# Linear attention and a routed MLP on one core: query transpositions on copied fp32r tiles, stacked tail keys, a new order table

## Chip, cores, metric

One core of a Trainium2 chip runs the whole program in one launch. The metric is device time in microseconds, as the median of several executions. The core has TensorE (PE; its weight loads are listed as PEld), VectorE (DVE), ScalarE (ACT), GpSimd (POOL) and SyncE (SP), which issues most DMAs.

## The reference

Eight heads of linear attention over eight sequences of 576 tokens, then a layer of eight experts in which each token goes to the one expert with the largest gate value:

```python
def phi(x):
    proj = np.einsum('bhsd,df->bhsf', x, w_phi)
    proj = proj - np.max(np.abs(proj), axis=-1, keepdims=True)
    return np.concatenate([np.exp(proj), np.exp(-proj)], axis=-1)
q_p, k_p = phi(q), phi(k)
kv = np.einsum('bhsf,bhsd->bhfd', k_p, v)
z = np.sum(k_p, axis=2)
num = np.einsum('bhsf,bhfd->bhsd', q_p, kv)
den = np.einsum('bhsf,bhf->bhs', q_p, z)[..., None] + 1e-06
x = (num / den)  # tokens x 512
expert_idx = np.argmax(x @ w_gate, axis=1)
for e in range(8):
    h = np.maximum(x[expert_idx == e] @ w1[e], 0.0)
    out[expert_idx == e] = gate_w[...] * (h @ w2[e])
```

All inputs and outputs are fp32.

## The kernel before

**Precision.** Products that must be exact to fp32 are made of fp32r operands: a tile is split into a high part (rounded to fp32r, written by ACT mostly) and a low part (the rest, written by DVE or POOL), and three products are added: high x high, high x low, low x high. Other products (`pn`, `pf`) and the transpositions take fp32 operands.

**Attention.** The work is cut into 16 units: four groups `g` of two sequences, and in each four pairs `pr` of heads. The tokens of a unit are nine pieces of 128 columns: eight of one sequence each and a ninth (number 8, the tail) that holds the last 64 tokens of both sequences. They are worked on in five steps, `PIECES`: the tail, then (0,1), (2,3), (4,5), (6,7). For each step and for `k` and `q`:

- `load` (L234) brings `xr` by an SP DMA, `split_high` and `split_low` make `xh` and `xl`; `project_steps` (L257) makes three products of 256 columns per piece into `ps_proj`; `project_max` (`mx`) and `project` (`t`, L282) are two DVE instructions.
- For keys, `k_features` (`e`), `k_high` (`kh`) and `k_low` (`kl`) follow on ACT, and on DVE or POOL.
- For queries, `q_turn_steps` (L315) transposes `t` in 128x128 blocks on PE into `pt`, as fp32, and `q_features` takes the exponentials of `pt` into `qp` or `qz` on ACT.
- `kv_steps` (L367) adds up `pk`, 65 output rows x 256 columns, over five pieces of one sequence `bb`, for two heads, with three products each (`kh` with `vh`, `kh` with `vl`, `kl` with `vh`): 30 per sequence and 60 per unit. For the tail piece the values of the other sequence are zero.
- `kv_copy`, `fold_steps` (`pf`), `num_steps` (`pn`, 73 columns, or 146 from the tail's `qz`), `normalize` and `store` end the unit.

**The order.** Each step of a unit has a letter (capitals for odd units), and the strings `HEAD`, `GROUP` and `TAIL` are the order in which all steps of all units are written into the program; each engine takes its share in that order. PE, DVE, ACT, POOL and SP all issue in order, and a step that waits holds what is behind it on its engine. The pools rotate their buffers.

**Experts.** Rows of `x_dram` are gathered in blocks of 128 (`xg`), transposed on PE into `px` (`x_parts`, L1128, four per block), split, and multiplied by `w1` (`pm`) and `w2` (`po`). 17 units take two blocks of one expert, the others one.

Of the kernel before, what the change touches and what calls it, by code (L numbers as in the profile page):

```python
# [12 lines left out]
I32 = mybir.dt.int32  # L13
# [52 lines left out]

@with_exitstack
def tile_linear_attention_moe(
# [18 lines left out]
    ident = keep.tile([P, P], F32, name="ident")  # L87
    make_identity(nc, ident)
# [13 lines left out]
    sm = late.enter_context(tc.tile_pool(name="sm", bufs=2, side="right"))  # L102
    sg = late.enter_context(tc.tile_pool(name="sg", bufs=1, side="right"))
    ps_kv = late.enter_context(tc.tile_pool(name="ps_kv", bufs=2, space=PSUM, side="right"))
    hold = mid.enter_context(tc.tile_pool(name="hold", bufs=1, side="right"))
    ps_nm = mid.enter_context(tc.tile_pool(name="ps_nm", bufs=2, space=PSUM, side="right"))
    inp = early.enter_context(tc.tile_pool(name="inp", bufs=1, side="left"))
    work = early.enter_context(tc.tile_pool(name="work", bufs=1, side="left"))
    kvp = early.enter_context(tc.tile_pool(name="kvp", bufs=1, side="left"))
    ps_pr = early.enter_context(tc.tile_pool(name="ps_pr", bufs=2, space=PSUM, side="left"))  # L110
    ps_tr = early.enter_context(tc.tile_pool(name="ps_tr", bufs=2, space=PSUM, side="left"))


    w_bd = const.tile([P, 2 * F], F32, name="w_bd")
# [4 lines left out]
    V.tensor_tensor(w_lo, w_bd, w_hi, op=ALU.subtract)  # L119


    one20 = const.tile([P, 2 * NC + 2, 1], F32, name="one20")
    V.memset(one20, 0.0)
    V.memset(one20[:, 0 : 2 * NC - 2], 1.0)
    V.memset(one20[0:D, 2 * NC - 2 : 2 * NC], 1.0)
    V.memset(one20[D:P, 2 * NC : 2 * NC + 2], 1.0)
# [22 lines left out]
    fold_parts += [lambda h=h: G.tensor_copy(fold[:, h, 0 : D + 1], ident[0 : D + 1, 0 : D + 1]) for h in range(H)]  # L149
# [27 lines left out]
    sel_p = rt.tile([P, NTILE, P], BF16, name="sel_p")  # L177
# [27 lines left out]
    CHUNKS = ((8, 0, 1, 2, 3), (4, 5, 6, 7, 8))  # L205
# [95 lines left out]
    def k_high(st, c0, n):  # L301
        m = 2 * n
        kh = kvp.tile([P, m, 2, F], F32R, name="kh", tag=f"kh{n}", bufs=3 * n - 1)
        A.copy(kh, st["e", c0][:, 0:m])
        st["kh", c0] = kh

    def k_low(st, c0, n):
        m = 2 * n
        kh = st["kh", c0]
        kl = kvp.tile([P, m, 2, F], F32R, name="kl", tag=f"kl{n}", bufs=3 * n - 1)  # L310
# [56 lines left out]
    def kv_steps(st, bb):  # L367


        def step(hh, i, c, j):  # L370
            vh, vl = v_tiles[st["u"] % 2]
            if (hh, i, j) == (0, 0, 0):
                st["pk", bb] = ps_kv.tile([P, 2, 2 * F], F32, name="pk", tag="pk")
            n = D if j == 1 else D + 1
            c0 = c if c == 8 else c - c % 2
            s0 = 2 * (c - c0)
# [3 lines left out]
                st["kl" if j == 2 else "kh", c0][:, s0 + hh].rearrange("p s f -> p (s f)"),  # L380
                start=(hh, i, j) == (0, 0, 0),
                stop=(hh, i, j) == (1, 4, 2),
# [6 lines left out]
            for j in range(3)  # L389
# [119 lines left out]
    def unit_items(st):  # L509
# [11 lines left out]
        for x in "kq":  # L521
            for c, n in PIECES:
# [97 lines left out]
    def route(g, lgc, c0, n, final=None):  # L620
# [96 lines left out]
        def count_step(c):  # L717
            oh_b, base_b = r["oh_b"], r["base_b"]
# [8 lines left out]
            else:  # L727
                T.matmul(r["prk"], ones, base_b.unsqueeze(1).to_broadcast([P, n, E]), start=False, stop=True)
# [190 lines left out]

    q_tail = [hold.tile([P, 2, 2, 2, D], F32, name=f"qz{i}") for i in range(2)]  # L920
# [7 lines left out]
    for g in range(NG):  # L928
# [9 lines left out]
    }  # L938
    HEAD = (
        "a0gb20B000000c0e212ahjd2g2ikk2jfjl2bk2D2n222m2pFKoKcssgtjje2haK22dMbjijjOqjljjuujfjjjhSSnATilkpkkkkn"  # L940
        "kGrckkkqkmkeuuuukopuurAjjjjCjjssslqsuEuuumuuutuunuuurapjjjjjjoduuuuqluufuuuunJJvJsuuLHrsBJwNsJJJJJJP"
        "JLJJJJwQsLwwICuNuuupuuNuuuukxkktJJkyUyyqRUgkkyEmyPUUuuyoUUyryaQsssysJJJtJJJLJJJJycULRyuuPuNuuuuuNuuu"
        "uuQuuuyUeKKPKKKKkkMUkUvkURkAUQkUwUUwUDmUwRUUhwOUUyUUoyUUPyxUsszsszyFzUKtKKUzyUKUyQiUbKKKKMKKVKKSyMcU"
        "SyUUOSWUSOWRSTGSSSjjjjjTljjjjnUWUlUpjjjejjnjqWUUXUpUKKlKbYUKrUYdUKUnYUqKfUYMUUYUpjjOUYUjrUAYCUjjUYqu"
        "jjjljjjjUdYluUEYuUnYuUYnuVuyuupfyauuWukkuHWruBkkkkkkkqWumIWumuyupuyXuyouyussoqySyukzrkgkzkkzkuCYSzum"
        "(YSyuZyouySyrZuTZyuyZuyuytSSzSSzvYzuEuzYzTszzY(zuYsYuYBuYsYuYsY(utJYuJYuJJJLJJJJNYuLYPuJYZuNJYQ(uJJZ"
        "YPRsJYuJZkwDukZYL)sQwuFkNwuYskPwuYxRsakkktkmkkkkyumYcuyouuQyueuoyuyuZyZuyZsZyZuRAJJJu)ysJuyZsZvJZJJJ"
        "hLJJJJUwL)sswtsUNiwsUyNsUPwUUxyUUyUtUyUKzK)UzyDzUGKKKKQzKMFKKUyOUUMPySSKRKbKOKyTUKKUyQMUUyUUyOUcUyRU"
        "UyUUyUUyUVUySUySUyeUSzyzUjzjSyUTzUy(UjjbjljjjjnUWUlUpjjjynUjqjjydlSKUWUprKySKnfWUyqUKWSKXUypASrKzKKz"
        "KMKKKTYzUUzYzUzzU(YzOCUUYUYMqUEYUYSOYUjj(jUYrSajUYSVjjjjHjljjjuWlSSWTSunIW(SuYnSupWuuXYuuYuTuYukZkuZ"  # L950
        "YgdZukkkkqZkmfkkuYouumpYsskrkBkokYtukkuYqmuuYuuYouCuYruuYuuYuuYuvuYsuYsuYEusZYZuJZJsYutZuY)uJJBJLJJ"
    )
    GROUP = (
        "JJNuwuLuPJJJYNuJQJJYDLskuwuPRkYskNFwuYQukwskxuYPasRkZkkZkmkkktyZuuZyZuZZu)yZocuuyuymQueyuy3syuJJ)Juy"
        "soAJuysvRJJJJhJJJJUwLsswtsLUiw)sUyNsUDwUUNytUUyxUUyU3PKKUFyGUKzK3KK4K4KQzK3Uy5zbU5UyUzPU3yRUMUyUMUyU"
        "QUyOUUOySSKK3TKKRKKycUMUyUUyOUVUySUySUy5UeSz7yzUjzjSyUTzUy(Ujjbjljjj7jnUWUlUpjjjynUjqjjydl7SKUWUprKy"
        "SKnfWUyqUK7WSKXUypASrKzKKzKMKKKTYzUUzYzUzzU(YzOCUUYUYMqUEYUYSOYUjj(jUYrSajUYSVjjjjHjljjjuWlSSWTSunIW"
        "(SuYnSupWuuXYuuYuTuYukZkuZYgdZukkkkqZkmfkkuYouumpYsskrkBkokYtukkuYqmu66uYu6o666666C6uYru3uY3uuYuuY4u"
        "uYuuY4suY5suY4usZY5ZuJZJs4Yu5ZuY)uJ4JJ5LJJJJNuvY5uLu4JJJY5NuJtJJw5sLkuwDuk5YNsPkwu5YPukwFskxuYQskZkk"
        "ZQkmkkkEyBZuuZyZtuZZu)yZouuyaucymuyuy4RsyuJRoJ)PJuysJuysJvJJJLJ4JJJUwLesDswsUNtw)sUyNsUwFtUAUxyUUyUU"  # L960
        "PyUbKzKUzyzUKQKKKzKMKKUyOQUURySSKKTKKyURMK4KUyUMUyPUUyOUUyUOUcyUUyQUeUyUUySVUySUhRybUSzyzUjzjSyUTzUy"
        "(UjjjljjjijnUWUlUpjjjynUjqjjydlSKUWUpKnfyGSKWUyqUKWSrKAUySXrKpKKzKMKKKYzUOTUYUUYzUzUzYCzUzY(zUMYqUYE"
        "SYOUjjjUYSjU(rYSVjajjjHjjjljuWSSlWTSuIWSnuYSudnW(uuYTuXuYuuYupkZkuZfYgZukkkkpZkmkkuYoBuumYqsskkkokYt"
        "ukrkuYqmuuYuuYouCuYuuYuuYruuYuvuYsuYsuYusZYZuJZJEsYutZuY)uJJJLJJB"
    )
# [445 lines left out]
```

## Time and profile before

| what | value |
|---|---|
| runs | 912.37, 911.63, 907.03 us; median 911.63 |
| the profiled execution | 909.77 us, of which its span 908.1 us |
| TensorE (products) | 882.9 us busy, 6703 instructions |
| TensorE (weight loads) | 824.9 us busy |
| DVE, ACT, POOL | 589.5, 611.2, 487.3 us busy |
| mean granted clock | 0.987 |

The span runs from the first to the last instruction of one execution. Products on PE overlap, so the busy time of PE says how often it had something in flight, and the distance between starts says what one product cost. All instructions of engines that are recorded for ordering carry line 59, that of the helper; the names of their tiles tell them apart. A row of the timeline may stand for several equal instructions (x2, x4).

### The profile page before, as it was taken

Reading aid. Unit: us, or ns where it says so; the run is one execution under the profiler, and the core shown is the slowest. Engines: PE = TensorE matmul, PEld = TensorE weight load, DVE = VectorE, ACT = ScalarE, POOL = GpSimd, SP = SyncE. Lnnn points to the kernel's source line nnn. Section 1 sums busy time; section 2 is a strip of 40 time slices with the busy share of each in tenths; the row PEclk is TensorE's granted clock in tenths of the full one; section 3 lists DMA queues with packets and bytes.
Section 4 is the critical chain, followed back from the end, with each engine's and each line's share of the span. In section 5 each row is a group of like instructions: output and inputs, shape, how many; then the busy total and the mean of one; then the engine's idle time right before and its main releaser. Section 6 shows DMA issues by size and latency. Waiting matters only on the chain. (4 is left out here: it accounts for less than half of the span.)

```text
span 908.1 us, 18331 instructions
## 1 busy us (share of the span) xinstructions
PE 882.9 (97%) x6703; PEld 824.9 (91%) x6703; DVE 589.5 (65%) x1075; ACT 611.2 (67%) x954; POOL 487.3 (54%) x332
## 2 busy tenths in 40 slices
PE   8999999999999999999999999999999999999994
PEld 6999999999999999998889999999999999987883
DVE  7777788787877788868754444444444444457950
ACT  7987888887898778844745555555555555568951
POOL 6976666776695677632543333333333333337641
PEclk8999999999999999999999999999999999999997
DMA  5243333333333341251342253522434634653100
GB/s 171 89 130 109 109 108 99 88 96 108 109 91 93 101 109 54 87 199 21 101 163 70 94 163 116 163 70 87 139 125 132 219 118 141 228 206 120 46 24 16
DMA packets 64621, 102.46 MB, mean 113 GB/s; under 512 B 10702, under 2 KB 28622, under 8 KB 64528
## 3 DMA queue, kind: packets, MB, share of 16 engines
q1 hardware_dynamic: 57136, 80.31, 28.4%
q0 software_dynamic: 6720, 20.80, 7.4%
q8 instruction: 54, 0.88, 0.4%
q14 instruction: 39, 0.32, 0.1%
q10 hardware_dynamic: 672, 0.15, 0.1%
HBM read 136.81 MB, written 20.26 MB: 173 GB/s over the span
## 5 line engine op out<-in xcount | busy, mean ns | idle before, releaser
L59 DVE TENSOR_TENSOR wl<-raw,wh 128x1024 fp32r<-128x1024 f32 x138 | 184.6, 1350 | 139.9 <-ACT wh L59 135.6
L59 ACT CAST wh<-raw 128x1024 fp32r<-128x1024 f32 x184 | 191.2, 1050 | 94.3 <-PE po L59 67.3
L59 POOL TENSOR_TENSOR wl<-raw,wh 128x1024 fp32r<-128x1024 f32 x46 | 113.4, 2470 | 172.2 <-ACT wh L59 167.0
L59 PE MATMUL pn<-kf,qp 128*128 128x73 f32 x1024 | 167.2, 251 | 0.2 <-DVE kf L59 0.2
L59 PE MATMUL pm<-xh,wh 128*128 128x256 f32 x544 | 154.6, 284 | 1.5 <-DVE hl L59 1.5
L59 PE MATMUL pm<-xl,wh 128*128 128x256 f32 x544 | 154.9, 285 | 1.2 <-DVE xl L59 1.2
L59 PE MATMUL pm<-xh,wl 128*128 128x256 f32 x544 | 154.7, 284 | 0.0
L59 PEld LDWEIGHTS pn<-kf,qp 128*128 128x128 f32 x1024 | 154.1, 189 | 0.5 <-DVE kf L59 0.4
L59 PE MATMUL po<-wh,hh 128*128 128x512 f32 x328 | 131.4, 401 | 0.3 <-ACT hh L59 0.3
L59 PE MATMUL po<-wl,hh 128*128 128x512 f32 x328 | 128.6, 392 | 0.0
L59 PE MATMUL po<-wh,hl 128*128 128x512 f32 x328 | 128.0, 391 | 0.6 <-DVE hl L59 0.6
L59 POOL TENSOR_TENSOR xl<-xr,xh 128x512 fp32r<-128x512 f32 (+2 forms) x63 | 91.6, 1456 | 61.0 <-ACT xh L59 57.3
L59 POOL TENSOR_TENSOR kl<-e,kh 128x1024 fp32r<-128x1024 f32 x47 | 112.7, 2406 | 20.0 <-ACT kh L59 10.9
L59 DVE TENSOR_REDUCE mx<-ps_proj 128x4 f32<-128x512 f32 (+1 forms) x160 | 99.9, 630 | 26.0 <-PE ps_proj L59 25.1
L59 PEld LDWEIGHTS pm<-xh,wh 128*128 128x128 f32 x544 | 104.9, 193 | 4.2 <-DVE hl L59 1.7
L59 PEld LDWEIGHTS pm<-xl,wh 128*128 128x128 f32 x544 | 104.9, 193 | 4.1 <-DVE xl L59 1.7
L59 PEld LDWEIGHTS pm<-xh,wl 128*128 128x128 f32 x544 | 104.8, 193 | 0.0
L59 DVE TENSOR_TENSOR t<-ps_proj,mx 128x512 f32<-128x512 f32 (+1 forms) x160 | 99.5, 634 | 5.5 <-ACT e L59 0.9
L59 PE MATMUL pk<-kh,vh 128*65 128x256 f32 x320 | 98.1, 307 | 0.5 <-ACT kh L59 0.5
L59 PE MATMUL pk<-kl,vh 128*65 128x256 f32 x320 | 97.7, 305 | 0.1
L59 PE MATMUL pk<-kh,vl 128*64 128x256 f32 x320 | 97.6, 305 | 0.0
L59 POOL DMA_INDIRECT out<-ob,sidx x41 | 44.5, 1086 | 91.1 <-ACT ob L59 81.2
(201 smaller groups left out, 2006.1 us busy)
## 6 DMA issues: line engine op xcount, KB each, us to landing
raw<-w SPq DMA_DIRECT2D x184, 512.0 KB
vt<-vv SPq DMA_DIRECT2D x15, 640.0 KB
x_dram<-xrow SPq DMA_DIRECT2D x30, 256.0 KB
xr<-qT SPq DMA_DIRECT2D x15, 320.0 KB
xr<-kT SPq DMA_DIRECT2D x15, 320.0 KB
xr<-kT SPq DMA_DIRECT2D x17, 256.0 KB
xr<-qT SPq DMA_DIRECT2D x17, 256.0 KB
x_dram<-xrow SPq DMA_DIRECT2D x32, 32.0 KB
```

The lines of the kernel that those rows point to most:

```text
L59: m = f(*a, **kw)
```

## The change

- Queries: a new step `q_move` (letters `[` and `]`) copies `t` into a tile `tq` by an SP DMA, and `q_turn_steps` transposes `tq` instead of `t`, with operands read as fp32r, through a helper `turn`. The gathered rows `xg` are transposed by `turn` too. The identity is written as fp32r.
- Tail keys: `k_stack_steps` (letters `{` and `}`) makes two tiles `ka`, one per sequence, by four SP DMAs: the sequence's 64 rows of `kh` stand on its own half of the partitions and its 64 rows of `kl` on the other. The host puts the tail values twice into `vv`, once on each half. For the tail, `kv_steps` then needs two products per head (`ka` with `vl`, `ka` with `vh`) instead of three.
- Order: `HEAD`, `GROUP` and `TAIL` are new, `GROUP` is used twice; the last 42 steps instead of 51 are spread into the first expert unit.
- Buffers: pools of the attention part are wrapped in `Ring`, in which a table names the buffer of each tile. There is one more pair of `kh` and `kl` buffers of two pieces.
- Some tiles of the index computation lie in a pool `spots`, opened when the pool `hold` is closed.

```diff
+class Ring:
+    def tile(self, shape, dtype, name, tag=None, bufs=None):
...
+        slots = self.slots.get(tag, "")
+        slot = slots[k] if k < len(slots) else k % n
+        return self.pool.tile(shape, dtype, name=name, tag=f"{tag}_{slot}", bufs=1)
...
-    CHUNKS = ((8, 0, 1, 2, 3), (4, 5, 6, 7, 8))
+    CHUNKS = ((0, 1, 8, 2, 3), (4, 5, 6, 7, 8))
...
+    def k_stack_steps(st):
+
+        def step(b, i):
+            if i == 0:
+                st["ka", b] = kvp.tile([P, 2, 2, F], F32, name="ka", tag=f"ka{b}", bufs=2)
+            own, other = (slice(D * x, D * x + D) for x in (b, 1 - b))
+            dst, src = (other, "kl") if i else (own, "kh")
+            return SP.dma_start(st["ka", b][dst], st[src, 8].bitcast(F32)[own])
+
+        return [lambda a=(b, i): step(*a) for b in range(2) for i in range(2)]
+
+    def q_move(st, c0, n):
+        m = 2 * n
+        st["tq", c0] = work.tile([P, 4, F], F32, name="tq", bufs=2)
+        SP.dma_start(st["tq", c0][:, 0:m], st["t", "q", c0][:, 0:m])
+
+    def turn(dst, src):
+
+        return T.transpose(dst.bitcast(F32R), src.bitcast(F32R), ident_r)
+
...
-            return T.transpose(st["pt", c0][:, i, :], st["t", "q", c0][:, i, :], ident)
+            return turn(st["pt", c0][:, i, :], st["tq", c0][:, i, :])
...
+            if c == 8:
+                keys = st["ka", bb].bitcast(F32R)[:, hh]
...
-            for j in range(3)
+            for j in ((1, 0) if c == 8 else range(3))
...
+        "tq": "01010110100101010101010101010101010101010101010101010101010101010101010101010101",
...
-            T.transpose(px[:, k, :], xg[:, k * P : (k + 1) * P], ident)
+            turn(px[:, k, :], xg[:, k * P : (k + 1) * P])
```

Where the order moves instructions: first PE, in a unit of the steady part. Before, transpositions into `pt` stand between single `pf`, `pn` and `pk` products:

```order
L59 MATMUL pk<-kh,vh_166 65x256
L59 MATMUL pf<-fold,kvT 128x73
L59 MATMUL pt<-ident,t 128x128 x2
L59 MATMUL pf<-fold,kvT 128x73
L59 MATMUL pt<-ident,t 128x128
L59 MATMUL pk<-kh,vl_168 64x256
L59 MATMUL pf<-fold,kvT 128x73
L59 MATMUL pt<-ident,t 128x128
L59 MATMUL pk<-kl,vh_166 65x256
L59 MATMUL pn<-kf,qp 128x73
L59 MATMUL pt<-ident,t 128x128
L59 MATMUL pk<-kh,vh_166 65x256
```

Now, at the like place:

```order
L59 MATMUL pk<-kh,vl_166 64x256
L59 MATMUL ps_proj<-w_lo,xh 128x256
L59 MATMUL pt<-ident_r,tq 128x128 x4
L59 MATMUL pk<-kl,vh_164 65x256
L59 MATMUL pk<-kh,vh_164 65x256
L59 MATMUL pf<-fold,kvT 128x73
L59 MATMUL pk<-kh,vl_166 64x256
L59 MATMUL pf<-fold,kvT 128x73
L59 MATMUL pk<-kl,vh_164 65x256
L59 MATMUL pf<-fold,kvT 128x73
```

The four transpositions of a pair of pieces stand together, and every `pf` now has a `pk` behind it. Up to the last `pn`, 260 of 296 transpositions are followed by another one or by a `pk`; before, 119 were.

Then SP, in the steady part. Before, its queue holds loads of `xr` and `vt` and stores of `xrow`:

```order
L59 DMA xr<-kT 128x640
L59 DMA x_dram<-xrow 64x128
L59 DMA vt<-vv 128x1280
L59 DMA xr<-qT 128x640
L59 DMA x_dram<-xrow 128x4x128
L59 DMA xr<-qT 128x512
L59 DMA x_dram<-xrow 64x128
L59 DMA xr<-kT 128x512
```

Now the copies stand between them:

```order
L59 DMA xr<-qT 128x512
L59 DMA x_dram<-xrow 128x4x128
L59 DMA ka<-kh 64x512
L59 DMA xr<-kT 128x512
L59 DMA ka<-kl 64x512
L59 DMA tq<-t 128x512
L59 DMA xr<-kT 128x640
L59 DMA tq<-t 128x512
L59 DMA tq<-t 128x256
L59 DMA x_dram<-xrow 64x128
```

Nine more DMAs per unit pass through SP: five into `tq` and four into `ka`. 17 of the 80 into `tq` stand directly behind a load of `xr` or `vt`, as one does here.

## Rows read from the trace of the kernel before

**Rows 1.** The page: busy us, share of the span, instructions, for TensorE.
```profile
PE 882.9 (97%) x6703; PEld 824.9 (91%) x6703; DVE 589.5 (65%) x1075; ACT 611.2 (67%) x954; POOL 487.3 (54%) x332
```

**Rows 2.** Windows: length, busy us per engine (instructions), granted clock, DMA share, GB/s.
```profile
0.00:25.00 25.00, 20.99 (x117) 16.67 (x118) 19.36 (x41) 18.23 (x33) 17.03 (x39) 0.86 0.57 166
100.00:150.00 50.00, 49.96 (x467) 49.64 (x466) 40.94 (x97) 39.24 (x68) 34.02 (x21) 1.00 0.37 105
150.00:200.00 50.00, 48.17 (x456) 47.79 (x454) 40.35 (x87) 44.17 (x83) 38.24 (x25) 1.00 0.33 93
500.00:550.00 50.00, 50.00 (x324) 45.59 (x323) 24.97 (x27) 27.62 (x36) 18.60 (x13) 1.00 0.36 117
```

**Rows 3.** Waits of PE: us in total, times, longest.
```profile
PE ps_proj L59 <- DVE t L59: 5.0, 5, 1.8
PE pm L59 <- DVE hl L59: 1.5, 1, 1.5
```

**Rows 4.** Timeline, weight loads, attention: start us, us, engine, line, operation, tiles, shape, count.
```profile
203.23 0.14 PEld L59 LDWEIGHTS pk<-kh,vh 128*65 128x65 f32 x1
203.29 0.14 PEld L59 LDWEIGHTS pk<-kh,vl 128*64 128x64 f32 x1
203.41 0.30 PEld L59 LDWEIGHTS pn<-kf,qp 128*128 128x128 f32 x2
203.64 0.14 PEld L59 LDWEIGHTS pk<-kl,vh 128*65 128x65 f32 x1
```

**Rows 5.** Products into `pn`: count, shortest, median, longest ns; first and last start.
```profile
L59 PE MATMUL pn<-kf,qp x1024: 224/272/357, 27.2 to 403.6; 128*128 128x73 f32 x171
L59 PE MATMUL pn<-kf,qz x128: 285/286/336, 62.4 to 404.6; 128*128 128x146 f32 x128
```

**Rows 6.** Timeline, weight loads around a block's transpositions in the expert part.
```profile
564.00 0.46 PEld L59 LDWEIGHTS px<-ident,xg 128*128 128x128 f32 x4
564.43 0.19 PEld L59 LDWEIGHTS po<-wh,hh 128*128 128x128 f32 x1
...
564.78 0.19 PEld L59 LDWEIGHTS po<-wh,hl 128*128 128x128 f32 x1
565.01 0.19 PEld L59 LDWEIGHTS po<-wh,hh 128*128 128x128 f32 x1
```

**Rows 7.** Timeline, weight loads around a transposition of queries.
```profile
104.41 0.19 PEld L59 LDWEIGHTS pt<-ident,t 128*128 128x128 f32 x1
104.52 0.14 PEld L59 LDWEIGHTS pk<-kh,vl 128*64 128x64 f32 x1
104.64 0.31 PEld L59 LDWEIGHTS pf<-fold,kvT 65*128 65x128 f32 x2
```

**Rows 8.** Groups of weight loads: count, busy us, mean ns of one.
```profile
L59 PEld LDWEIGHTS pm<-xh,wh 128*128 128x128 f32 x544 | 104.9, 193 | 4.2 <-DVE hl L59 1.7
...
L59 PEld LDWEIGHTS pk<-kl,vh 128*65 128x65 f32 x320 | 44.2, 138 | 0.5 <-DVE kl L59 0.3
...
L59 PEld LDWEIGHTS px<-ident,xg 128*128 128x128 f32 x164 | 19.1, 141 | 1.0 <-DMA xg<-x_dram,gidx 0.8
```

**Rows 9.** Load of 256 KB: issue; DMA, 218.6 to 222.6 in 40 slices; a store's landing.
```profile
218.60 0.33 SPq L59 DMA_DIRECT2D xr<-kT  x1
GB/s 0 0 0 0 0 0 0 0 0 102 225 102 184 205 102 184 348 348 266 307 144 61 21 21 0 0 0 0 5 123 164 36 0 0 174 302 292 292 292 287
x_dram<-xrow POOLq DMA_DIRECT2D x2, 256.0 KB, 3.3
```

**Rows 10.** Groups on DVE: the two steps behind a projection.
```profile
L59 DVE TENSOR_REDUCE mx<-ps_proj 128x4 f32<-128x512 f32 (+1 forms) x160 | 99.9, 630 | 26.0 <-PE ps_proj L59 25.1
L59 DVE TENSOR_TENSOR t<-ps_proj,mx 128x512 f32<-128x512 f32 (+1 forms) x160 | 99.5, 634 | 5.5 <-ACT e L59 0.9
```

**Rows 11.** Waits of SP's queue: us in total, times, longest.
```profile
SPq L59 <- POOL xl L59: 136.4, 47, 9.1
```

More of the change, by code (lines that the diff above doesn't have):

```diff
@@ L64, in __getattr__, with __init__ @@
         return call
+class Ring:
+    def __init__(self, pool, bufs=1):
+        self.pool, self.bufs, self.count = pool, bufs, {}
+        self.slots = {}
+    def tile(self, shape, dtype, name, tag=None, bufs=None):
+        tag, n = tag or name, bufs or self.bufs
+        if n == 1:
+            return self.pool.tile(shape, dtype, name=name, tag=tag, bufs=1)
+        k = self.count.get(tag, 0)
+        self.count[tag] = k + 1
+        slots = self.slots.get(tag, "")
+        slot = slots[k] if k < len(slots) else k % n
+        return self.pool.tile(shape, dtype, name=name, tag=f"{tag}_{slot}", bufs=1)
 @with_exitstack
@@ L86, in tile_linear_attention_moe @@
     xgp = ctx.enter_context(tc.tile_pool(name="xgp", bufs=4, side="left"))
-    ident = keep.tile([P, P], F32, name="ident")
-    make_identity(nc, ident)
+    ident_r = keep.tile([P, P], F32R, name="ident_r")
+    ident = ident_r.bitcast(F32)
     gidx = keep.tile([P, NB], I32, name="gidx")
@@ L148, in tile_linear_attention_moe @@
     fold_parts = [lambda: G.memset(fold, 0.0)]
-    fold_parts += [lambda h=h: G.tensor_copy(fold[:, h, 0 : D + 1], ident[0 : D + 1, 0 : D + 1]) for h in range(H)]
+    fold_parts += [lambda h=h: G.tensor_copy(fold[:, h, 0 : D + 1], eye[0 : D + 1, 0 : D + 1]) for h in range(H)]
     def load_gate():
@@ L176, in tile_linear_attention_moe @@
     blk = rt.tile([P, NTILE], F32, name="blk")
-    sel_p = rt.tile([P, NTILE, P], BF16, name="sel_p")
     sel_h = rt.tile([P, NTILE, P], BF16, name="sel_h")
@@ L302, in k_high @@
         m = 2 * n
-        kh = kvp.tile([P, m, 2, F], F32R, name="kh", tag=f"kh{n}", bufs=3 * n - 1)
+        kh = kvp.tile([P, m, 2, F], F32R, name="kh", tag=f"kh{n}", bufs=4 * n - 3)
         A.copy(kh, st["e", c0][:, 0:m])
@@ L309, in k_low @@
         kh = st["kh", c0]
-        kl = kvp.tile([P, m, 2, F], F32R, name="kl", tag=f"kl{n}", bufs=3 * n - 1)
+        kl = kvp.tile([P, m, 2, F], F32R, name="kl", tag=f"kl{n}", bufs=4 * n - 3)
         eng = G if c0 in (4, 6) or (c0 == 0 and st["u"] > 0) else V
@@ L727, in count_step @@
             else:
-                T.matmul(r["prk"], ones, base_b.unsqueeze(1).to_broadcast([P, n, E]), start=False, stop=True)
+                held = r["base_b"].unsqueeze(1).to_broadcast([P, n, E])
+                T.matmul(r["prk"], ones, held, start=False, stop=True)
         def own_ranks():
@@ L944, in tile_linear_attention_moe @@
[L944 to L948, printed above, removed]
@@ L1001, in tile_linear_attention_moe @@
             queues.setdefault(letters[st["u"] % 2], []).append(f)
-    plan = [queues[c].pop(0) for c in HEAD + 1 * GROUP + TAIL]
-    nums = plan[-51:]
+    plan = [queues[c].pop(0) for c in HEAD + 2 * GROUP + TAIL]
+    nums = plan[-42:]
     V.on = A.on = G.on = T.on = SP.on = True
-    run(plan[:-51])
+    run(plan[:-42])
     V.on = A.on = G.on = T.on = SP.on = False
@@ L1033, in block_of @@
         V.tensor_single_scalar(at, at, 63, op=ALU.bitwise_and)
-        bi = sg.tile([P, NTILE], F32, name="bi")
+        bi = spots.tile([P, NTILE], F32, name="bi")
         V.tensor_tensor(bi, blk, turn, op=ALU.is_ge)
@@ L1054, in tokens_of @@
         V.tensor_scalar(gidx, pp, -1.0, 0.0, op0=ALU.add, op1=ALU.max)
-        emp = sg.tile([P, NB], F32, name="emp")
+        emp = spots.tile([P, NB], F32, name="emp")
         V.tensor_scalar(emp, pp, 0.5, BIG, op0=ALU.is_lt, op1=ALU.mult)
@@ L1059, in experts_of @@
     def experts_of():
-        ends = sg.tile([1, 2, E], F32, name="ends")
+        ends = spots.tile([1, 2, E], F32, name="ends")
         G.tensor_tensor(ends[:, 0], first[0:1], paired[0:1], op=ALU.add)
@@ L1063, in experts_of @@
         V.tensor_reduce(nblk, ends[:, 1], axis=AX.X, op=ALU.max)
-        eg = sg.tile([1, 2, NB, E], F32, name="eg")
+        eg = spots.tile([1, 2, NB, E], F32, name="eg")
         places = ((first[0:1], ends[:, 0], 0, 2 * NPAIR), (start[0:1], ends[:, 1], 2 * NPAIR, NB))
@@ L1246, in tile_linear_attention_moe @@
     weights(0, 1)
-    run(nums[16:36])
+    run(nums[16:27])
     run(r1[:1])
-    run(nums[36:])
+    run(nums[27:])
     weights(0, 3)
@@ L1256, in tile_linear_attention_moe @@
     mid.close()
+    spots = late.enter_context(tc.tile_pool(name="spots", bufs=1, side="right"))
+    bsel = spots.tile([P, NTILE, NB], BF16, name="bsel")
     ps_t = ctx.enter_context(tc.tile_pool(name="ps_t", bufs=2, space=PSUM, side="left", reuse_waits="tile"))
@@ L1384, in rows @@
         tail = a[..., 4 * P :, :].transpose(0, 2, 1, 4, 3, 5).reshape(NG * NPR, P, 2, D)
-        res = np.zeros((NG * NPR, P, 2 * NC + 2, D), a.dtype)
+        res = np.empty((NG * NPR, P, 2 * NC + 2, D), a.dtype)
         res[:, :, 0:16] = main
-        res[:, 0:D, 16:18] = tail[:, 0:D]
-        res[:, D:P, 18:20] = tail[:, D:P]
+        for b in range(2):
+            half = tail[:, D * b : D * b + D]
+            res[:, :, 16 + 2 * b : 18 + 2 * b] = np.concatenate([half, half], axis=1)
         return res
```

156 lines of the change are left out of this document (93 added, 63 removed), and 5 rows, old and new, of the table LETTERS.

## Prediction

> **What bounds the kernel now.** I read the page first: TensorE (PE) is busy 97% of the span and its weight loads (PEld) 91% [rows 1]. A busy PE is not proof of a full one, so next came the windows [rows 2]: from 100 to 150 us PE, 49.96 of 50 us, never stands, the two vector engines (DVE, ACT) work about 80% and GpSimd (POOL) 68%; in the expert part (500 to 550) PE has all 50 us and the others are half idle. The granted clock is 1.00, the 2.4 GHz level, in both. Only the first 25 us show a PE that waits (20.99 busy), with the clock at 0.86. The waits confirm it: the largest PE wait, on DVE's `t`, sums to 5.0 us in 5 times [rows 3]. So a change is worth what it takes out of PE's own sequence, less new waits.
>
> What one product costs there stands in the weight loads in order of time. A load starts when the product before its own starts, so from one load to the next passes the longer of two things: that product's streaming and the load. In [rows 4] a 65-column load behind a 73-column fp32 product (203.23 to 203.29) takes 0.065 us; behind it comes a 256-column fp32r product, 0.12 (203.29 to 203.41); then two 128-column loads fill 0.23, of which 0.12 lie under the second such product and 0.11 under the short `pn` product. The expert part gives a 512-column fp32r product 0.23 [rows 6]. So I count, in us: fp32r products of 256 columns 0.118; a short fp32 product (0.065 by itself) followed by a 128-column load 0.110, followed by a `pk` load 0.065. An fp32 product of `pn` or `pf` is two such records (1,024 records [rows 5] for 512 products in the program's order); a transposition is one (288).
>
> The transposition: in [rows 7] the load of `pk` (65 columns, which takes 0.065 at most) follows the load of `pt` by 0.11, and 0.12 pass to the load behind it (104.52 to 104.64), under the transposition: its 128 fp32 columns therefore stream for about 0.11 themselves. In the expert part four loads of `px` and the next stand 0.108 apart (0.43 for four) [rows 6].
>
> As a check I laid these costs over PE's order in the program, up to the last `pn`: 1,824 long products x 0.118 = 215.2; 1,280 short records, 828 x 0.110 + 452 x 0.065 = 120.5; 128 records of `qz` at 0.124 (146 columns, twice the 73) = 15.9; 296 transpositions x 0.110 = 32.6; small ones 6.6. Sum 390.8. The last `qz` stands at 404.6 [rows 5]; PE's idle time and half clock at the start take most of the difference of 14. The sum holds, and I use it for the change.
>
> **The change, part by part.**
>
> *Stacked tail keys.* High and low part of the tail keys lie on the two halves of one tile `ka`, and the values are there twice, so the tail's 3 products per head become 2: 4 fewer per unit, 64 in all. 64 x 0.118 = -7.6 us. The two copies into each half are DMAs; in the order PE has at least 2.6 us of products between the copies and their first reader in the first unit and 3.5 in the others, against a transfer of about 2.4 us (below): hidden; if transfers collide and take 3.3, the first unit alone loses 0.7.
>
> *New order.* What counts is what stands behind a short record: 0.045 us less if it is a 65-column load. Before, 452 of 1,280 are followed by one; now 570, because a `pn` stands alternately with a `pk` and the transpositions no longer sit between. 709 x 0.110 + 570 x 0.065 = 115.0 against 120.5: -5.4 us. This assumes nothing of the chip that [rows 4] don't show.
>
> *Transpositions as fp32r.* The trace has no fp32r transposition. Upper bound: as now, 0.110, no gain. Lower bound: the load alone. Transposing loads last 141 ns in the expert part, as `pk`'s 65-column ones do with 138, where other 128-column loads last 193 [rows 8]; so 0.065, as with `pk`. For the streaming, columns decide: 256 more fp32r columns cost 0.23 - 0.12 = 0.11, that is 0.43 ns each, an fp32 column 0.065/73 = 0.89. 128 fp32r columns: 0.055. I take 0.065 wherever the next instruction is another transposition or a `pk`, and 0.110 where a 128-column load follows. The order decides how many: it puts the transpositions in fours (second fence of the order), so of 296 up to the last `pn`, 260 are followed by a short load, 35 by a long one. 260 x 0.065 + 35 x 0.110 = 20.8 against 32.6: -11.8. Gathered rows: 156 more transpositions run in the expert part, in fours, three of each four followed by another: 117 x 0.045 = -5.3. The fourth gains nothing, as the 128-column load of `po` follows.
>
> The Trainium skill has a rule against this: the glossary ("Terms") of "TensorE: Matmul & The Clock Gate" puts a transpose mode on trn2 that is 4 times faster for fp32, and "TensorEngine Tiling (Array Packing)", "Gotcha 2", names fp32 and fp32r inputs of that mode together. By that fp32 has the fast mode already and this part is worth 0; the first rival is that case, priced there from rows. The trace leaves it open: 0.11 per 128 columns is the fp32 rate of `pn`, not the fp32r one.
>
> *The copy.* fp32r operands are copied from `t` to `tq` by an SP DMA first: 80 copies of up to 256 KB, a new step in the chain from projection to transposition. The nearest row is a load of the same size and shape: issued at 218.60, its bytes end 23 or 24 tenths later [rows 9], 2.4 us; a 256 KB store on POOL's queue lands after 3.3. A copy from SBUF to SBUF is not in the trace, nothing excludes that it is quicker than a load; bounds 1 and 3.3, I take 2.4. In the order the tightest of the five pieces of a unit has, between its last projection and its first transposition, 14 projections, 13 `pk` and 9 `pn` products: 27 x 0.118 + 9 x 0.175 = 4.8 us. The chain: drain 0.28, `mx` 0.63, `t` 0.63 [rows 10], copy 2.4: 3.9. Spare 0.9; with 3.3 it is level. So no wait in the steady part if DVE and the SP queue are prompt. In the first unit the tail's two transpositions have under 1 us of cover: +2. For the rest I put +3 (16 units x 0.2). A wait on PE holds everything behind it, as PE takes its products in order: +5 in all; from -6 (no new wait, and places such as the 1.8 us that PE loses between 150 and 200 [rows 2] gone with the new order) to 15. The copy itself waits on SP for `t` and for PE to free `tq`; behind it stand loads and stores of later steps, whose readers are many us away.
>
> *The rest.* Ring tables only name the buffer of each tile; `one20` and the identity move a few short DVE instructions of the start; the index tiles moved to the freed pool are used after it is freed. 0. The copies bring 80 x up to 256 KB and 64 x 128 KB, some 27 MB in 390 us, 68 GB/s beside 105 at a DMA share of 0.37 [rows 2]: about 0.6, hidden.
>
> Sum on the profiled execution (909.8 us, span 908.1): -7.6 - 5.4 - 11.8 - 5.3 + 5 = -25.1, so 884.7. That execution is 1.9 below the median of the runs (911.6); on the median 886.5.
>
> **The rivals.**
>
> *1. fp32r transposes no faster.* Then 0.110 stays: -13.0 + 5 = -8.0, 903.6 us. For it: no row has an fp32r transposition; the load and the streaming of `px` both fit into 0.108 and can't be told apart there. Against it: 65-column and `px` loads last alike, and 0.11 is what the fp32 column rate makes.
>
> *2. Slower: the copies queue on SP behind loads.* SP issues in order, and a load waits until POOL's `xl` has freed its buffer: 136.4 us in 47 times, 2.9 us on average, 9.1 the longest [rows 11]. That cost nothing while only loads stood there. Now 17 of the 80 copies stand directly behind a load (fourth fence). If one copy per unit is held 2.9 us, the 0.9 of spare leave 2.0 on PE: 16 x 2.0 = 32, 918.5 us; with two copies 950. From 1.6 us per unit on, the gain is gone. Against it: such loads run ahead of need, and the order puts them where POOL should be done; POOL is 68% busy.
>
> *3. ACT becomes late at the ends of groups.* In 150 to 200 us it has 44.17 us of work in 50 [rows 2] and PE already loses 1.8 there; 390 us that shrink by 25 make 88% into 94%. If each of four such places loses 3 us more, +12: 898.5.
>
> **How the numbers follow.** My forecast 0.62, its own range 876 to 896 (waits -6 to 15). First rival 0.20, third 0.08, second 0.10. A measurement here tells about 1% from no change, so the line is 902.5 us. Faster: nearly all of the forecast and the third rival and some of the first, 0.77; within 1%: most of the first, 0.13; slower: the second, 0.10. The range 874 to 907 takes in the first and third rival and leaves out the second.
>
> **What would show it.** Right: PE's windows stay full in the steady part, the last `qz` near 380; the group of `pt` transpositions with a mean start-to-start of 0.065 in fours; four `px` loads spread over about 0.3 us instead of 0.43; 896 products into `pk`. Wrong: `px` loads still 0.108 apart (first rival); PE waits on `DMA tq` of over 1 us once per unit with SP waiting for POOL `xl` just before (second); PE waits for ACT's `qp` or `kh` every fourth unit (third). The forecast is wrong if attention ends after 392.

## The result, and the profile after

| | before | after |
|---|---|---|
| runs | 907.03 to 913.22, median 911.64 us (6) | 897.98 to 904.7, median 900.29 us (6) |
| ratio | | 0.9885, 95% interval 0.985 to 0.9919 |
| the profiled execution, its span | 909.77, 908.1 us | 898.09, 896.4 us |
| last product into `pn` | 404.6 us | 392.6 us |

The change gains 11.4 us where 25.1 were forecast. The time lies outside the forecast's own range (876 to 896) and inside the wide one (874 to 907), 3 us from the place of the first rival (903.6), but it came about by another mechanism.

The page and the windows after, for [rows 1] and [rows 2] (length, busy us of PE, PEld, DVE, ACT, POOL, granted clock, DMA share, GB/s):

```profile
PE 865.8 (97%) x6639; PEld 806.9 (90%) x6639; DVE 580.1 (65%) x1073; ACT 608.0 (68%) x954; POOL 487.1 (54%) x332
```
```profile
0.00:25.00 25.00, 19.74 (x111) 16.82 (x112) 18.46 (x39) 17.90 (x31) 18.14 (x39) 0.80 0.69 205
100.00:150.00 50.00, 50.00 (x490) 49.81 (x489) 42.26 (x105) 42.06 (x76) 35.89 (x22) 1.00 0.62 186
150.00:200.00 50.00, 48.80 (x460) 48.08 (x459) 38.86 (x87) 46.48 (x86) 40.35 (x26) 1.00 0.57 176
```

PE is as full as before; its products got cheaper, 490 instead of 467 in the same 50 us. The DMA share went from 0.37 to 0.62.

The products of queries end earlier, but later than the 380 that the forecast named (for [rows 5]):

```profile
L59 PE MATMUL pn<-kf,qz x128: 285/286/336, 48.7 to 392.6; 128*128 128x146 f32 x128
```

PE's waits, for [rows 3], have a new first line, the copies:

```profile
PE pt L59 <- DMA tq<-t: 3.3, 6, 1.0
PE ps_proj L59 <- DVE t L59: 3.1, 3, 1.9
PE pm L59 <- DVE hl L59: 2.7, 1, 2.7
```

The weight loads around four transpositions in the attention part (for [rows 7]) and in the expert part (for [rows 6]):

```profile
110.32 0.14 PEld L59 LDWEIGHTS pk<-kh,vh 128*65 128x65 f32 x1
110.43 0.43 PEld L59 LDWEIGHTS pt<-ident_r,tq 128*128 128x128 f32 x4
110.81 0.13 PEld L59 LDWEIGHTS pk<-kh,vl 128*64 128x64 f32 x1
110.86 0.31 PEld L59 LDWEIGHTS pn<-kf,qp 128*128 128x128 f32 x2
...
506.66 0.41 PEld L59 LDWEIGHTS px<-ident_r,xg 128*128 128x128 f32 x4
507.02 0.19 PEld L59 LDWEIGHTS po<-wh,hh 128*128 128x128 f32 x1
507.12 0.19 PEld L59 LDWEIGHTS po<-wl,hh 128*128 128x128 f32 x1
```

Read as in the prediction: the first `pt` load lasts 0.12 under the product before it, and the three others share the rest of the 0.38 (110.43 to 110.81), about 0.085 each. From the load of `pk` behind them to the next pass 0.05 (110.81 to 110.86; the median of 55 such places is 0.056): neither that load nor the streaming of the last transposition takes longer. So the columns of an fp32r transposition pass as fast as forecast (0.055), but its load takes 0.085 and not 0.065. Over the trace the median of 199 such loads behind another transposition is 0.085 (0.110 before), and of 38 behind a short `pn` or `pf` product 0.133, where an fp32 one took 0.110.

To compare kernels I gave each weight load the time to the next one that its product and load cost where nothing waits (the prices of the prediction and those just read, 0.110 for fp32 transpositions), and call what is left lost. In us, up to the last `pn` and behind it:

| | attention: products | lost | experts: products | lost |
|---|---|---|---|---|
| before | 387.9 | 15.5 | 481.9 | 9.4 |
| after | 367.2 | 24.2 | 479.9 | 11.8 |
| difference | -20.7 | +8.7 | -2.0 | +2.4 |

The four differences sum to -11.6; the spans differ by 11.7. Each row is one execution, and the runs of one kernel spread by 2 to 11 us, so a difference of one or two us in the lost time of two kernels is not told apart by such rows alone.

### The profile page after: what moved, and what is told of

Read it like the earlier page. It is cut to its first block, busy times and chain, and to the rows that moved or that the text cites. A ratio compares the mean times of both kernels' runs of the same rounds, so it can differ in the third digit from the quotient of the medians.

```text
span 896.4 us, 18565 instructions
## 1 busy us (share of the span) xinstructions
PE 865.8 (97%) x6639; PEld 806.9 (90%) x6639; DVE 580.1 (65%) x1073; ACT 608.0 (68%) x954; POOL 487.1 (54%) x332
## 5 line engine op out<-in xcount | busy, mean ns | idle before, releaser
L59 PE MATMUL pn<-kf,qp 128*128 128x73 f32 x1024 | 156.6, 253 | 0.0
L59 PEld LDWEIGHTS pn<-kf,qp 128*128 128x128 f32 x1024 | 151.1, 190 | 0.1
L59 ACT ACTIVATE e<-t 128x512 f32<-128x512 f32 (+1 forms) x160 | 85.4, 592 | 8.1 <-DVE kl L59 3.4
L59 PE MATMUL ps_proj<-w_hi,xh 128*128 128x256 f32 x288 | 84.1, 294 | 6.3 <-DVE t L59 3.1
L59 DVE SCALAR_TENSOR_TENSOR hl<-pm,hh 128x512 fp32r<-128x512 f32 x68 | 46.7, 687 | 61.5 <-ACT hh L59 61.5
```

Of the source, the lines that this page charges most:

```text
L59: m = f(*a, **kw)
```

## Experiments

All in one table; "us" is the median, "last `pn`" is the start of the last product into it, "lost" is the sum just described, in the attention part and in the expert part. Ratios are to the kernel before on the same chip.

| run | us | ratio, 95% interval | last `pn` | lost |
|---|---|---|---|---|
| px_alone | 912.82 | 1.002, 1.0006 to 1.0034 | 406.5 | 16.8, 14.9 |
| px_back | 899.44 | 0.9888, 0.9856 to 0.992 | 391.9 | 23.3, 10.2 |
| copy_fp32 | 903.67 | 0.9908, 0.9878 to 0.9938 | 401.0 | 25.9, 11.9 |
| no_copy_fp32 | 895.8 | 0.9831, 0.9804 to 0.9859 | 391.5 | 16.4, 11.5 |
| no_stack | 905.17 | 0.991, 0.9879 to 0.9942 | 395.3 | 12.7, 15.8 |
| no_copy_px32 | 898.91 | 0.9852, 0.9827 to 0.9878 | 390.6 | 15.4, 10.9 |
| copy_unread | 901.13 | 0.9865, 0.9836 to 0.9895 | 390.1 | 15.1, 18.5 |
| copy_on_act | 915.62 | 1.0038, 1.001 to 1.0065 | 402.6 | 34.1, 15.6 |
| more_cover | 902.69 | 0.9907, 0.9871 to 0.9943 | 396.8 | 27.5, 13.7 |
| no_copy_no_pool | 894.14 | 0.9823, 0.979 to 0.9857 | 391.2 | 16.1, 8.9 |
| changed_no_pool | 897.04 | 0.9833, 0.9795 to 0.9871 | 394.0 | 25.6, 9.1 |
| copy_where_covered | 895.09 | 0.982, 0.9791 to 0.985 | 390.8 | 19.7, 9.9 |
| copy_late_units | 890.54 | 0.9776, 0.9762 to 0.9789 | 387.8 | 16.4, 8.8 |

**The gathered rows, alone and undone.** px_alone is the kernel before with an identity copied into an fp32r tile and

```diff
-            T.transpose(px[:, k, :], xg[:, k * P : (k + 1) * P], ident)
+            T.transpose(px[:, k, :].bitcast(F32R), xg[:, k * P : (k + 1) * P].bitcast(F32R), ident_r)
```

and px_back the changed kernel with this line undone.

> The kernel before with one part of the change: the gathered rows are transposed as fp32r (and the identity is copied once into an fp32r tile). Theory A (an fp32r transposition streams in 0.055 us, but its weight load costs 0.085 behind another transposition): px loads 0.085 apart instead of 0.109, 122 pairs x 0.024 = 2.9 us less, about 908.7 us against 911.6. The price of the prediction (0.065): 122 x 0.044 = 5.4 us, 906.2. If fp32r did nothing: 911.6.

> The changed kernel with the gathered rows transposed as fp32 again. Theory A: px loads 0.109 apart, 2.9 us more than the changed kernel (900.3): 903.2, ratio to before 0.991. The prediction's price: 905.6.

The loads of `px` stand 0.086 apart in the one and 0.109 in the other, so the transposition is faster. The products of the expert part fall by 3.7 us in the one (481.9 to 478.2) and rise by 2.9 in the other, but neither time shows it: alone it is 0.2% slower, with 5.5 us more lost behind the last `pn`. The forecast had 5.3. From the distances themselves, 122 loads at 0.023 us less give an estimate of 2.8.

**The query part taken apart.** copy_fp32 keeps the copies and transposes `tq` as fp32; no_copy_fp32 has no copies, transposes `t` as fp32 and holds it in six buffers instead of four:

```diff
-            return turn(st["pt", c0][:, i, :], st["tq", c0][:, i, :])
+            return T.transpose(st["pt", c0][:, i, :], st["t", "q", c0][:, i, :], ident)
```

> The changed kernel in which the query copies tq stay but are transposed as fp32. Theory A: behind another transposition 0.110 instead of 0.085 (199 pairs, 5.0 us), before a pk 0.110 instead of 0.055 (55, 3.0 us), behind a short fp32 product 0.110 instead of 0.133 (38, 0.9 us less): 7.1 us more than the changed kernel, 907.4, ratio 0.9953. The prediction's price (0.065): 11.8 us more, 912.1. PE waits on the copies stay at 3 to 5 us, as the copies are as late.

> The changed kernel without the query copies: t itself is transposed as fp32, in the same order, with six buffers of t instead of four of t and two of tq. Theory A: transpositions cost 7.1 us more than in the changed kernel, but the 4.6 us of waits for copies go: about 902.8, ratio 0.9903. Rival (the copies cost more than PE's own waits show, by holding SP and other transfers): below 900, faster than the changed kernel. Rival (the copies cost nothing): 907.4 as with the copies kept.

Without copies the kernel is faster than the changed one, by 0.5% of the time before, with intervals that overlap at their ends (0.985 and 0.9859). Between the two runs the copies add 9.5 us of lost time in the attention part (16.4 to 25.9); between copy_fp32 and the changed kernel, fp32r takes 6.7 us off its products (373.9 to 367.2). Against no_copy_fp32 the changed kernel has 7.8 us more of lost time and 6.7 us less of products: the pair costs a little more than it brings. (The profiled execution of copy_fp32, 906.8 us, is the slowest of its four, so that the 9.5 may be high; its ratio, 0.9908, is not told apart from the 0.9885 of the changed kernel.) PE's waits in copy_fp32:

```profile
PE pt L59 <- DMA tq<-t: 7.5, 6, 1.5
PE pm L59 <- DVE hl L59: 2.6, 1, 2.6
```

**Stacked keys and order.** no_stack is no_copy_fp32 with three products per head for the tail again, without the copies into `ka`, with the tail values once and two buffers each for the tail's `kh` and `kl` as before; no_copy_px32 is no_copy_fp32 with `px` as fp32. The core of the edit of no_stack:

```diff
-            return SP.dma_start(st["ka", b][dst], st[src, 8].bitcast(F32)[own])
+            return None
...
-            return T.matmul(
+            m = T.matmul(
...
+            return step(hh, i, c, 2) if c == 8 and j == 1 else m
```

(So the third product stands directly beside the second in the order.)

> The version without copies (t transposed as fp32, 895.8 us), and without the stacked tail keys: three products per head for the tail piece again, the third beside the second in the order, values of the other sequence zero as before, two buffers for the tail's kh and kl. What is left of the change is the new order, the buffer tables and the gathered rows. By the sum, 64 products of 0.118 us come back: +7.6, so 903.4 us; against the kernel before (911.0) that leaves -7.6 for the order, of which 5.4 were forecast. Rival (the freed PE time of the stacked keys went into waits, and the order brought all of it): 896 to 899 us.

> The version without copies, and the gathered rows transposed as fp32 again: stacked tail keys and the new order alone, with t in six buffers. If the transposition of gathered rows is hidden by waits on their gathers, as the runs with it alone (ratio 1.002) and without it (0.9888 against 0.9885) have it, 895 to 897 us; if 122 loads at 0.086 instead of 0.109 us count, +2.8: 898 to 899 us.

The products of the attention part are 387.9 before, 381.5 with the new order alone, 373.9 with the stacked keys too: 6.4 for the order (5.4 forecast) and 7.6 for the keys (7.6). Both together are no_copy_px32, 1.5% faster than before, or 13.5 us for the 13.0 of the forecast. This half of the prediction held as a sum, and in part by luck. Its two parts go different ways when the waits are counted, by one execution of each: up to the last `pn` the order brought 9.3 us (404.6 to 395.3, with 2.8 less lost) and the keys 3.8 (395.3 to 391.5), because 3.7 of their 7.6 us went into lost time (12.7 to 16.4). Where those waits come from stays open. The 9.4 us between the medians of no_stack and no_copy_fp32 hold 4.3 us of lost time in the expert part (15.8 against 11.5), which the edit does not touch.

**Why a copy costs.** copy_unread is no_copy_fp32 with all copies issued again, but nobody reads them; `t` has five buffers instead of six:

```diff
-        return None
+        st["tq", c0] = work.tile([P, 4, F], F32, name="tq", bufs=1)
+        SP.dma_start(st["tq", c0][:, 0:m], st["t", "q", c0][:, 0:m])
```

copy_on_act is the changed kernel with `A.dma_start` in place of `SP.dma_start` in `q_move`.

> The 80 copies into tq are still issued at their places on SP (one tq buffer instead of two), but nobody reads them: PE transposes t itself as fp32, t has five buffers. The run with copies and fp32 transpositions took 903.67 us, the one without copies 895.8. Theory 1 (PE waits for the copies to land): unread copies cost nothing, so 894 to 898 us, PE's waits in the attention part back at about 16 us. Rival (the copies' traffic and their places in SP's queue delay loads and the vector engines, whoever reads them): 901 to 905 us, PE's waits there near 25 us with DVE's t and POOL's xl as releasers.

> The changed kernel with one edit: the copies into tq are issued by ACT instead of SP, at the same place in the order. Theory A (a copy is late because it stands in SP's queue, behind loads that wait for POOL's xl or behind the packets of a 320 or 640 KB load): it lands sooner, PE's 9 us of added waits fall by half or more, 892 to 897 us. Theory B (the transfer itself, about 4 us beside other traffic, is longer than the cover): no difference, 899 to 902 us. Theory C (ACT, in order, is held at the copy until DVE has written t, and its kh and qp come late): 903 us or more, with PE waits on ACT.

By the time alone, 901.13, the rival would have won. The attention part says otherwise: it ends at 390.1 with 15.1 us lost, as without copies. So their traffic and their places in SP's queue hold nobody up there; what costs is to read them. (The number of buffers of `t` differs too, but neither here nor in the changed kernel does DVE wait for one.) The 5 us of the whole run lie in the expert part (18.5 lost), where nothing was changed; two pairs of runs below take that up. On ACT the copies made PE wait for them longer:

```profile
PE pt L59 <- DMA tq<-t: 10.4, 13, 1.3
```

That is no help to theory A. The time, 915.62, is that of theory C, but the waits on ACT that it named stay small (1.6 us for `xh`, 1.1 for `kh`), so what else makes this kernel slow stays open.

How late a copy is, the changed kernel shows where PE had to wait (start, length, engine, and in brackets what ended an idle time):

```profile
173.56 0.33 SPq L59 DMA_DIRECT2D xr<-kT  x1
173.60 0.68 DVE L59 TENSOR_TENSOR t<-ps_proj,mx 128x512 f32<-128x512 f32 x1
174.35 0.48 SPq L59 DMA_DIRECT2D tq<-t  x1
174.88 0.59 SPq L59 DMA_DIRECT2D ka<-kl  x1
...
178.63 0.53 PE L59 MATMUL pt<-ident_r,tq 128*128 128x128 f32 x4 [0.84 <-DMA tq<-t]
```

SP issued the copy 0.07 us after DVE ended `t`, so SP's queue did not hold it; in four of the five such places of the changed kernel it is 0.06 or 0.07. 4.3 us pass from issue to the first transposition. It was not alone on the DMA engines: a load of `xr` was issued 0.79 us ahead of it and a copy into `ka` 0.53 us behind, and from 174.3 to 177.0 us they moved 0.65 MB (241 GB/s), of which 0.26 are this copy. How long it would take alone no run shows. Where PE waited over 0.3 us for a copy, in this kernel and in copy_fp32, it is 3.4 to 4.9, mostly 4.3 to 4.7 (the 4.0 of the expectations was read from fewer places). The forecast had 2.4, bounded at 3.3 by a store.

**The same copies with more cover.** more_cover moves 31 groups of transpositions, with their exponentials, to later places in the order:

```diff
-    plan = [queues[c].pop(0) for c in HEAD + 2 * GROUP + TAIL]
+    plan = [queues[c].pop(0) for c in PLAN]
```

> The changed kernel with only its order edited: 31 of the 80 groups of query transpositions (with the exponentials that read them) stand later, so that by the sum of products at least about 7 us, instead of 4.9 to 7, lie between the last projection of a piece and its transposition, as far as the first product that reads the result leaves room. Theory 1 (the copies land 4.0 to 4.9 us after their issue, later than the order's cover): most of the 9 us of added waits in the attention part go, it ends at 383 to 386 instead of 392.5, and the time is 890 to 894 us. Rival (the waits come from elsewhere: SP held, DVE or ACT late): 898 us or more; if the exponentials are now late for the products behind them, PE waits on ACT's qp and the time is above 902 us.

A miss, with the time of the expectation's last case, though the wait is on `kvT` and not on `qp`. PE's waits for `tq` fell from 3.3 to 1.4 us, but the exponentials that moved along stand in front of `kvT` on ACT, and PE's loads now wait there (below, of more_cover). Lost time rose to 27.5. This order had no room for the steps that moved; another one was not tried.

```profile
PE pt L59 <- DMA tq<-t: 1.4, 2, 0.9
PEld ps_proj L59 <- DVE t L59: 4.3, 6, 2.1
PEld pm L59 <- DVE xl L59: 3.9, 1, 3.9
PEld pf L59 <- ACT kvT L59: 3.6, 10, 0.8
```

**DVE and POOL.** The lost time at the start of the experts differs between kernels that are the same there. The timeline of copy_unread, and then of no_copy_fp32, at the like place:

```profile
441.45 2.48 POOL L59 TENSOR_TENSOR wl<-raw,wh 128x1024 fp32r<-128x1024 f32 x1 [5.44 <-ACT wh L59]
441.62 3.39 DVE L59 TENSOR_TENSOR wl<-raw,wh 128x1024 fp32r<-128x1024 f32 x1
...
446.27 0.58 PE L59 MATMUL pm<-xl,wh 128*128 128x256 f32 x1 [3.55 <-DVE xl L59]
```
```profile
442.62 1.21 DVE L59 TENSOR_TENSOR wl<-raw,wh 128x1024 fp32r<-128x1024 f32 x1
442.67 3.40 POOL L59 TENSOR_TENSOR wl<-raw,wh 128x1024 fp32r<-128x1024 f32 x1 [4.52 <-ACT wh L59]
...
445.08 0.38 PE L59 MATMUL pm<-xl,wh 128*128 128x256 f32 x1 [1.36 <-DVE xl L59]
```

Where POOL starts first, by 0.17 us, DVE's step ends 1.08 us after POOL's (441.45 + 2.48 = 443.93; 441.62 + 3.39 = 445.01) and PE waits 3.55 us for the `xl` behind it; where DVE is first, by 0.05, POOL's step is the long one and PE waits 1.36. The Trainium skill has the rule ("SBUF — State Buffer", section "SBUF: two separate sides"): VectorE with two SBUF inputs and GpSimd share a port pair, and whichever starts first has it for its whole instruction. The traces agree, with the 1.08 us. no_copy_no_pool and changed_no_pool take POOL out of these steps:

```diff
-    POOL_LO0, POOL_LO = (1, 3), (3, 7)
+    POOL_LO0, POOL_LO = (1, 3), ()
```

> The version without copies (ratio 0.9831 to before), with the low parts of the expert weights written by DVE alone from the second unit on; POOL wrote two of eight before. In the traces a DVE step of this kind that starts while POOL is in one ends 1.1 us after POOL's end, taking 3.4 us instead of 1.2, and PE then waits for xl behind it on DVE: 1.4 us at 443 in one run, 3.5 us in others, by which of the two engines starts first. Theory (these meetings of DVE and POOL are what is lost at the start of the experts): the waits there and near 825 us fall by 2 to 4 us, ratio 0.979 to 0.982. Rival (DVE's own load sets it): no change, 0.982 to 0.985, or slower with PE waits on DVE's hl and wl.

> The changed kernel with the one edit of the run no_copy_no_pool (894.14 us): low parts of the expert weights on DVE alone from the second unit on. It takes the meetings of DVE and POOL out of the comparison, so that only the query part differs between the two: copies and fp32r transpositions here, neither there. If the copies' waits and the cheaper transpositions cancel, as the profiled ends of attention (392.5 against 391.3) have it, 894.5 to 896.5 us; if the copies cost more than fp32r gives back, as the medians of whole runs had it (900.29 against 895.8), 897 to 900 us; if fp32r were worth its forecast, 888 us.

PE from 425 to 450 us in copy_unread, no_copy_fp32 and no_copy_no_pool:

```profile
425.00:450.00 25.00, 21.45 (x132) 19.35 (x132) 21.69 (x16) 14.48 (x18) 10.58 (x5) 0.91 0.35 110
```
```profile
425.00:450.00 25.00, 23.64 (x158) 21.39 (x158) 21.50 (x18) 15.89 (x20) 12.10 (x6) 1.00 0.33 109
```
```profile
425.00:450.00 25.00, 25.00 (x169) 23.03 (x168) 20.36 (x21) 17.35 (x23) 4.15 (x4) 1.00 0.31 106
```

The wait is gone with the meeting, and 2.6 us of lost time in the experts (11.5 to 8.9). copy_unread itself was not run without POOL in these steps, so that all of its 18.5 us come from such meetings is not shown. The two ratios of the kernels without copies overlap, so the gain in time is shown by the traces alone. With these meetings out of the way, copies with fp32r still bring nothing: 0.9833 against 0.9823, last `pn` at 394.0 against 391.2.

**Copies only where they are covered.** copy_where_covered is changed_no_pool with

```diff
+        if (st["u"], c0) in DIRECT:
+            return None
...
+            if (st["u"], c0) in DIRECT:
+                return T.transpose(st["pt", c0][:, i, :], st["t", "q", c0][:, i, :], ident)
```

where `DIRECT` names 29 of the 80 pieces. copy_late_units adds units 0 and 1 to `DIRECT` (32 pieces) and has five buffers for `t` instead of four, tabled anew, and one for the first `ka`.

> The changed kernel with two edits: the 29 of 80 pieces whose copy has the least cover in the order (under 6.9 us of products since the last projection, or under 5 us since t, among them piece 4 of nearly every unit) are transposed from t directly as fp32, the other 51 are copied and transposed as fp32r; and the expert weights' low parts are written by DVE alone from the second unit on. Theory 1 (late landings of the tight copies are the added waits): the sum of products rises by some 2.7 us to 369.5, the waits of the attention part fall from 24.7 to about 16.5 as without copies, it ends near 386 us, 5 before the version without copies, and the time is 888 to 891 us. Rival (any copies cost, by their places in SP's queue or their traffic): waits stay at 22 or more, 895 to 898 us.

> As copy_where_covered, but without copies in units 0 and 1 (48 copies left, 170 of 296 transpositions as fp32r), with five buffers for t, tabled so that none is written again for 6 us of products after its copy was issued, and one buffer instead of two for the first sequence's ka to make room. In copy_where_covered DVE's t waited 3.5 us at 26 us until a copy had read its buffer. Theory 1 (a copy costs by landing some 4 us after its issue, at its reader and at the buffer it reads, and by nothing else): the waits of the first 75 us go back to 15 us as without copies, those behind stay at 2 to 3, attention ends at 386 to 388 and the time is 889 to 892 us, below the 894.14 us without copies. Rival (copies cost wherever they stand): 894 us or more.

The time of the first, 895.09, is at the edge of the rival's range, its lost time, 19.7, between the two expectations. Behind 75 us its lost time is 1.3 (after: 6.2; without copies: 1.0), as theory 1 has it; before, there is a new wait, on DVE:

```profile
29.69 0.69 DVE L59 TENSOR_TENSOR t<-ps_proj,mx 128x512 f32<-128x512 f32 x1 [3.46 <-DMA tq<-t]
```

DVE could not write `t` again before a copy had read it. DVE's list of copy_late_units no longer has that wait, and copy_late_units loses 16.4 us in the attention part, as much as without copies (16.1), while its products cost 370.3 instead of 373.9: 3.6 us, and 890.54 against 894.14 us is 3.6. No wait for a copy is left among its PE waits:

```profile
PE pm L59 <- DVE hl L59: 2.7, 1, 2.7
PE ps_proj L59 <- DVE t L59: 2.3, 3, 1.4
PE pw L59 <- DVE ones L59: 1.2, 1, 1.2
```
```profile
L59 PE MATMUL pn<-kf,qz x128: 285/286/336, 48.5 to 387.8; 128*128 128x146 f32 x128
```

So a copy costs by landing late, at its reader and at the buffer that it reads. copy_late_units, which also leaves POOL out of the low parts of the weights from the second unit on, is faster than both kernels: 2.2% than the one before.

## Why the prediction was right in direction and wrong in size

The forecast was 25.1 us, the profiled executions differ by 11.7. Term by term, on PE's own sequence:

| step of the prediction | forecast | measured |
|---|---|---|
| stacked tail keys | -7.6 | -7.6 |
| new order | -5.4 | -6.4 |
| query transpositions as fp32r | -11.8 | -6.7 |
| gathered rows as fp32r | -5.3 | -2.0 |
| waits, attention | +5 | +8.7 |
| waits, experts | 0 | +2.4 |

- *Right:* the two steps that rest on rows of the trace alone, the price of a product by columns and what stands behind a short record. Also the streaming of an fp32r transposition, 0.055. The prediction put no waits on the stacked keys beyond 0.7 us; no_stack against no_copy_fp32 shows 3.7, which the order's 2.8 less of lost time nearly hid.
- *The step that failed first:* "Transposing loads last 141 ns in the expert part, as `pk`'s 65-column ones do with 138 [...]; so 0.065, as with `pk`". Two loads whose records last alike need not follow each other alike. In fours they cost 0.085; behind a short fp32 product 0.133, dearer than the 0.110 of before. 8.4 us of the shortfall of 13.4 lie here and in its repetition for the gathered rows (7.5 if these count with the 2.9 of px_back; the -2.0 of the table is the difference of all products of the expert part). The upper bound of 0.110 was in the prediction, the value was taken from the wrong neighbour. Rival 1, no faster at all, falls with the 0.085. The rule weighed beside it in the prediction, by which fp32 already has the fast mode, does not hold for these instructions: the same tile takes 0.110 as fp32 and 0.085 as fp32r.
- *The second:* "bounds 1 and 3.3, I take 2.4" for the copy, and with it a spare of 0.9 us. The copies that PE waited for landed 3.4 to 4.9 us after issue, outside the bounds: a load's bytes on their way [rows 9] and a store's landing were no bound for a copy, in windows that move 176 to 186 GB/s in all. The chain of 3.9 us becomes 4.9 to 6.4 against a cover of 4.8, and +5 became 8.7, of which 7.8 are the difference to the kernel without copies. About 1.4 of these are no wait: PE stood 1.92 us for `t` at 61.93, and the same products took about 1.4 us longer behind it than in no_copy_fp32. From 60 to 66 us the granted clock is 0.72 in the changed kernel, in part the 1.2 GHz level, and 1.00 in no_copy_fp32, where PE stood 1.48 us at that place.
- *Rival 2* had the place of this wait and not its cause: SP was free when it issued the copy above, and SP's waits for POOL's `xl` [rows 11] fell from 136.4 to 58.5 us (the line below). *Rival 3*, ACT late at the ends of groups, did not come by the change; ACT was late, on `kvT`, when the transpositions were moved (more_cover).

```profile
SPq L59 <- POOL xl L59: 58.5, 41, 5.7
```

- *The waits in the expert part* were forecast at nothing. Half of the +2.4 is one wait, PE's for `hl` at the start of the experts, 1.5 us in [rows 3] and 2.7 above. All thirteen experiments have it at 2.4 to 2.9, px_alone with the old order and no copies among them, so neither the copies, the new order nor the later meetings of DVE and POOL can be its only cause; it stays open. By which of DVE and POOL is first, 1.4 or 3.5 us are lost at another place, and the traces show both for kernels that do not differ there. How much of the rest is that, one execution of each can't tell.
- By its own mark, "wrong if attention ends after 392", the forecast was wrong: 392.6.

One sentence of the part on the change is wrong: there is no additional pair of `kh` and `kl` buffers of two pieces. These stay at five each, and those of the tail go from two to one, and PE reads them only as they were copied into `ka`.

## What to carry to other kernels

Price an instruction that the trace doesn't have by its start-to-start distance in the nearest place, never by how long its record lasts, and keep the upper bound until a run has shown better. A DMA put into a chain can cost what its landing exceeds the spare at two places, at its reader and at the buffer that it reads; give it only to the pieces that have that time, and count it beside the traffic that will be there. When a change saves products, measure what is left of the saving at the end of the part as well: here half of one saving went into waits. Where time moves in a part that was not changed, look for two engines whose order of arrival is a coin toss before explaining it by the change.

## What was not expected of the hardware

- An fp32r transposition's load takes 0.085 us, a `pk` load 0.055 or less, though their records last 0.14 both; behind a short fp32 product the former takes 0.133.
- Copies of up to 256 KB within SBUF, where PE waited for them in the changed kernel and in copy_fp32, landed 3.4 to 4.9 us after issue.
- A DVE step with two SBUF operands that started behind a POOL step and met it ended 1.08 us after it, whatever its start; 0.05 to 0.17 us decided which of the two was held. In the attention part the changed kernel shows it too, and PE waits for the `t` behind it. The kernel without copies has this meeting as well (`kl` 3.14 us on DVE).

```profile
57.15 2.38 POOL L59 TENSOR_TENSOR kl<-e,kh 128x1024 fp32r<-128x1024 f32 x1 [0.56 <-ACT kh L59]
57.29 3.32 DVE L59 TENSOR_TENSOR kl<-e,kh 128x1024 fp32r<-128x1024 f32 x1
...
61.93 0.58 PE L59 MATMUL ps_proj<-w_hi,xh 128*128 128x256 f32 x1 [1.92 <-DVE t L59]
```

- After PE's wait of 3.55 us in copy_unread the granted clock of those 25 us was 0.91 (0.50, the 1.2 GHz level, from 446 to 450 us), after one of 1.36 us it was 1.00.
